# One step later for tanh, chunk 1's rows turned by transfers, weights requested and squared later (fused attention and MLP, one core)

## The chip, the cores and the metric

The kernel runs on one core of a Trainium2 chip. Its engines work side by side, each on its own list of instructions in order: PE (TensorE) multiplies matrices, ACT (ScalarE) and DVE (VectorE) work element by element, POOL (GpSimd) does small jobs, and SP (SyncE) issues most of the transfers. The metric is the device time of one execution in microseconds (us); lower is better.

## The reference, cut to what matters

```python
xn = layernorm(x)                                  # x: 2048 tokens x 640
q, k, v = split(xn @ wqkv)                         # 32 heads of 20
p = softmax(q @ k.T * 20 ** -0.5)                  # per head, 2048 x 2048
A = (p @ v).reshape(2048, 640) @ wo
h = gelu(layernorm(xn) @ w1 + b1)                  # 640 -> 1536, tanh form
out = x + A + h @ w2 + b2
```

## The kernel before

Everything is float32 in the reference. The kernel writes a float32 matrix as a sum of two 16-bit matrices (a "hi" and a "lo" part, after a scale that is a power of two), and multiplies with three matmuls: hi by hi, hi by lo, lo by hi (`PASS`). The scales come from sums of squares: ACT squares a weight matrix and adds up along the rows (L97, L464 for w2, L472 for w1, L483 for wo, L527 for Wq), PE multiplies the sums by a matrix of ones (`pow2`, L113), which adds over the 128 partitions, and a few one-column operations of DVE make a power of two of it (L114 to L119, L101, L423).

**Stage A, 0 to about 217 us**, takes the tokens in four chunks of 512 (c = 0 to 3). The order of the instructions is the one in which the program records them. For each chunk: its four tiles of 128 rows are loaded (`load_x`, L181); DVE takes mean and variance (`norm_a`, L243 to L245), scales the rows (`norm_b`, L258) and prepares the second layernorm's factor, which goes to a DRAM scratch, rscr (`norm_c`, L274). The rows are then turned, so that features lie on partitions, and split into hi and lo (xnt). For chunks 0 and 1, PE turns them (L537 and L541 for chunk 0; `transp`, L287, for chunk 1), and ACT and DVE copy them out of PSUM (L294, L295). For chunks 2 and 3 `turn` does it: ACT and DVE split the rows as they lie (L306, L307; three row buffers), and a DMA on SP transposes them (L308). SP stores each turned chunk to DRAM (xscr, L297 or L311) for the MLP.

With xnt, PE computes five tiles of q and k (`qk`, L325, 30 matmuls each), which ACT and DVE bring out of PSUM (L340, L341) and SP stores (qkscr, L346), and four tiles of v (`vproj`, L398; out by L408, L410). q, k and v tiles and the sums over partitions share three PSUM buffers (pool psS) in turn, so a tile waits until what stood in its buffer three allocations ago is read. In chunk 0 the columns of Wv are split (L431, L432) only after the fourth q/k tile.

Into this, two generators are cut in slices. `ask(n)` issues the next n loads of the MLP's weights on SP: six pieces of w2 of 640 KB, then five of w1 of 768 KB; chunk 0 asks for (0, 1, 2, 2, 1) behind its five q/k tiles and (2, 1, 1, 1) behind its four v tiles, and then for chunk 2's x. `some(n)` does the next n units of work on them: six squares of w2, scale "2", five squares of w1, scale "1", factors (with the square of b1), twelve splits of w2, fifteen of w1 (L128 to L130). In chunks 0 to 2 it does two behind each v tile, and in chunks 1 to 3 one or two behind each q/k tile.

**Stage B, from about 217 us,** is the attention. For each pair of heads, half of the queries and block of 128 keys, PE computes scores (L711), ACT takes the exponential (L713), DVE splits it where needed (L725), and PE multiplies by v (L742). After 16 blocks ACT evicts the sum (`ev`, L763), and transfers take it to DRAM. Between these, PE does the MLP (L976, L1006) and the projection by wo (z, L1090) as filler, by a credit in time. The element-wise work of the filler (gelu: a chain of DVE operations with a tanh on ACT) is a set of generators that advance by one step at every `tick`, two per group of four key blocks. `finish` turns the sums of a few heads into the attention's output: DVE adds up the denominators and takes reciprocals (L876 to L883), they are spread over the heads' rows, and DVE multiplies (L900 to L906); the result goes through DRAM (oscr) to the projection (ot, L1042).

**The tail** begins when the last scores are done, at about 1268 us. There are two chunks' worth of z matmuls left over, and `finish` for the last heads spreads the reciprocals with 32 matmuls (rb, L892), whose operand is not known until the last `ev` came back by a transfer. W1 sets how many ticks behind the loads the DVE chain and rb are recorded, a tick per three z matmuls; W2 how many ticks lie between rb and its reader (L900). The last 240 z matmuls (eight tiles of 30) read what this `finish` stores to oscr.

Of the kernel before, what the change touches and what calls it, by code (L numbers as in the profile page):

```python
# [9 lines left out]
F32 = mybir.dt.float32  # L10
# [8 lines left out]
P = 128  # L19
# [25 lines left out]
def mha_mlp_kernel(tc, x, wqkv, wo, w1, b1, w2, b2, out):  # L45
# [4 lines left out]
    with (  # L50
# [52 lines left out]

        def pow2(acc, tag):

            lo = keep.tile([P, 1], F32, name=f"lo_{tag}")
            hi = keep.tile([P, 1], F32, name=f"hi_{tag}")
            if tag in ("q", "k"):
                pt = psM.tile([P, 512], F32, tag="m", name="mxp")
            else:  # L110
                pt = psS.tile([P, 2, 512], F32, tag="s", name="mxp")[:, 0, :]
            n = acc.shape[1]
            nc.tensor.matmul(pt[:, :n], ones, acc, start=True, stop=True)  # L113
            nc.vector.tensor_reduce(lo, pt[:, :n], AX.X, ALU.add)  # L114
            nc.vector.tensor_scalar(lo, lo, 2.0**-100, 2.0**120, ALU.max, ALU.min)

            nc.vector.tensor_scalar(lo.bitcast(I32), lo.bitcast(I32), 0x7F000000, 1,
                                    ALU.bitwise_and, ALU.logical_shift_right)
            nc.vector.tensor_scalar(lo, lo, 2.0**64, None, ALU.mult)  # L119
            exponents(lo, hi)  # L120
            return lo, hi

        pw = {}

# [39 lines left out]
        with tc.tile_pool(name="pa", bufs=2) as pa, tc.tile_pool(name="pa1", bufs=1) as pa1, tc.manual_schedule():  # L164
# [21 lines left out]
            nc.gpsimd.memset(ones, 1.0)  # L186
            nc.gpsimd.memset(nhalf, -0.5)
            nc.gpsimd.memset(half, 0.5)
            load_x(0)
# [36 lines left out]
            def newton(dst, v, pref, by=1.0):  # L226
                t = pa.tile([P, 4], F32, tag=pref + "t", name=pref + "t")
                nc.vector.tensor_mul(t, dst, dst)
                nc.vector.tensor_mul(t, t, v)
                nc.vector.tensor_scalar(t, t, -0.5 * by, 1.5 * by, ALU.mult, ALU.add)  # L230
                nc.vector.tensor_mul(dst, dst, t)

            def norm_a(c, between=None):

                xt = xts[c]
                st = pa.tile([P, 4, 2, 6], F32, tag="st", name="st")
                mv = pa.tile([P, 4, 2], F32, tag="mv", name="mv")
                ve = pa.tile([P, 4], F32, tag="ve", name="ve")
                r = pa.tile([P, 4], F32, tag="r", name="r")
                r2 = pa.tile([P, 4], F32, tag="r2", name="r2")  # L240
                for j in range(4):
                    for i in range(2):
                        nc.vector.bn_stats(st[:, j, i, :], xt[j][:, i * 320 : (i + 1) * 320])  # L243
                    nc.vector.bn_aggr(mv[:, j, :], st[:, j])
                nc.vector.tensor_scalar(ve, mv[:, :, 1], EPS, None, ALU.add)  # L245
                if c == 0:
                    between()
                    nc.scalar.activation(r, ve, AF.Sqrt)
# [27 lines left out]
            xnts = {}  # L276

            def transp(c, k0, pts):
                if k0 == 0:
                    xnts[c] = pa.tile([P, KD, 2, 512], F16, tag="xnt", name=f"xnt{c}")  # L280
                if k0 + 2 > KD:
                    pt = psM.tile([P, 512], F32, tag="m", name="pt4")[:, None, :]
                else:
                    pt = psS.tile([P, 2, 512], F32, tag="s", name="pt")
                for j in range(4):
                    for k in range(min(2, KD - k0)):
                        nc.tensor.transpose(pt[:, k, j * P : (j + 1) * P],  # L287
                                            xts[c][j][:, (k0 + k) * P : (k0 + k + 1) * P], ident)
                pts.append((c, k0, pt))

            def transp_out(c, k0, pt):
                nk = min(2, KD - k0)
                ks = slice(k0, k0 + nk)
                nc.scalar.activation(xnts[c][:, ks, 0, :], pt[:, :nk], AF.Copy)  # L294
                nc.vector.tensor_sub(xnts[c][:, ks, 1, :], pt[:, :nk], xnts[c][:, ks, 0, :])  # L295
                if k0 + 2 > KD:
                    nc.sync.dma_start(xscr[:, :, :, c * 512 : (c + 1) * 512], xnts[c])  # L297
                    del xts[c]

# [114 lines left out]
            junk = pa1.tile([P, 3 * D], BF16, name="junk")  # L414
            accs, scales = {}, {}

            def sums(tag, ws):
                accs[tag] = squares(ws, junk)

            def scale_of(tag):  # L420
                pw[tag] = pow2(accs[tag], tag)
                scales[tag] = keep.tile([P, 1], F32, name=f"s_{tag}")
                nc.vector.tensor_scalar(scales[tag], pw[tag][1], 4096.0, None, ALU.mult)  # L423
                if tag in "qk":
                    q = "qk".index(tag)
                    nc.vector.tensor_scalar(qks[:, q : q + 1], pw[tag][0], QKTOP, 2.0**-22, ALU.min, ALU.mult)

# [93 lines left out]
            nc.scalar.activation(junk[:, :1], ones[:, :1], AF.Sqrt)  # L521
            warm(37)
            accs["q"] = sm.tile([P, 8], F32, tag="acc", name="acc")[:, :KD]
# [9 lines left out]
            pts = [psS.tile([P, 2, 512], F32, tag="s", name="pt") for _ in range(2)]  # L533
            pt = [pts[0][:, 0], pts[0][:, 1], pts[1][:, 0], pts[1][:, 1]]
            for j in range(4):
                for k in range(KD - 1):
                    nc.tensor.transpose(pt[k][:, j * P : (j + 1) * P], xts[0][j][:, k * P : (k + 1) * P], ident)  # L537
            scale_of("q")
# [3 lines left out]
            warm(3)  # L542

            for k in range(KD):
                nc.scalar.activation(xnts[0][:, k, 0, :], pt[k], AF.Copy)
                nc.vector.tensor_sub(xnts[0][:, k, 1, :], pt[k], xnts[0][:, k, 0, :])
                split_qkv("q", [k], 0, 2 * P)
            nc.sync.dma_start(xscr[:, :, :, :512], xnts[0])
            del xts[0]
            nc.gpsimd.dma_start(bscr[H : H + 1, :].rearrange("h (r t) -> h r t", r=4), brow[0:1, None, :].to_broadcast([1, 4, S // 4]))  # L550
            nc.gpsimd.dma_start(b1t, b1.rearrange("(k p) -> p k", p=P))
            for c in range(4):
                nxt = c + 1 if c < 3 else None
                for tt in range(5):
# [14 lines left out]
                    if c == 0:  # L569
# [22 lines left out]

                    ask((0, 1, 2, 2, 1)[tt] if c == 0 else 0)
                    if nxt and c > 0 and tt >= 2:
# [36 lines left out]
        with ExitStack() as scope:  # L631
# [278 lines left out]
            def gelu(ps, r2f, hT, f):  # L910
# [55 lines left out]
            def layer1(mc, f):  # L966
# [4 lines left out]
                for i in range(2):  # L971
                    n = 0
                    fo_ = (f + i) % 4 * P
                    for k in range(KD):
                        for a, b in PASS:
# [3 lines left out]
                            if n % 3 == 0:  # L979
                                if i == 1 and n == 15:  # L980
                                    begin(gelu(ps, r2f, hTs[mc], f))
                                yield 0.3276
# [72 lines left out]
            def ahead():  # L1055
# [3 lines left out]
                load_piece(0)  # L1059

            done = [False]
            ended = [False]
            W1, W2 = 10, 5

# [55 lines left out]
            with tc.manual_schedule():  # L1120
# [50 lines left out]
                n = 0  # L1171
                ended[0] = True
                fetch_results()
# [111 lines left out]
```

## Time and profile before

| | us |
|---|---|
| median of 3 runs | 1339.41 |
| lowest, highest | 1338.3, 1340.97 |
| the profiled execution | 1340.0 |
| its span, first to last instruction | 1338.0 |
| PE busy | 1328.0 |
| ACT busy | 1128.4 |
| DVE busy | 1055.1 |

The span is what the profile covers; about 2 us of the execution lie outside it. A group's row gives the busy time, the mean length of one instruction in ns and, behind the bar, the idle time of the engine ahead of it with what ended it. A row of the chain gives start, length, engine and line. A row of a table of windows gives, for each engine, busy time and instructions, then TensorE's granted clock, the DMA engines' busy share and GB/s. SPq and POOLq are transfers issued on those queues.

### The profile page before, as it was taken

How to read it: one execution, taken by the hardware profiler on the slowest of the kernel's cores; microseconds unless marked ns; L12 is line 12 of the kernel's file. 1: busy time of each engine (PE TensorE's matmuls, PEld its weight loads, DVE VectorE, ACT ScalarE, POOL GpSimd, SP SyncE). 2: the span in 40 equal slices, each digit the busy share in tenths (PEclk: the TensorE clock that was granted, in tenths of full speed). 3: DMA queues.
4: the chain of work that ended last, by engine and by line, in shares of the span. 5: the costliest groups of instructions: out<-in, count | busy, mean ns of one | idle time of the engine just before them, and what ended most of it. 6: DMA issues, size and time to landing. Idle time of an engine off the chain costs nothing.

```text
span 1338.0 us, 29071 instructions
## 1 busy us (share of the span) xinstructions
PE 1328.0 (99%) x11647; PEld 590.0 (44%) x11647; DVE 1055.1 (79%) x1436; ACT 1128.4 (84%) x1306; POOL 37.5 (3%) x85
## 2 busy tenths in 40 slices
PE   9999999999999999999999999999999999999998
PEld 6645545443434343444443444434343434333366
DVE  7767935998788888878897888898888888997632
ACT  7755525999999999999999999999999999999900
POOL 3011000000000000000000000000000000000000
PEclk9999999999999999999999999999999999999989
DMA  8767831121122223122322041322022323443465
GB/s 279 251 200 184 147 106 58 34 57 39 49 69 68 80 57 103 41 71 57 110 66 71 19 112 48 95 72 71 19 80 72 95 65 85 128 134 80 122 189 189
DMA packets 100150, 129.54 MB, mean 97 GB/s; under 512 B 24276, under 2 KB 66328, under 8 KB 100012
## 3 DMA queue, kind: packets, MB, share of 16 engines
q1 hardware_dynamic: 96652, 120.25, 30.7%
q0 software_dynamic: 2912, 6.90, 2.8%
q8 instruction: 92, 1.51, 0.5%
q10 hardware_dynamic: 448, 0.51, 0.2%
q14 instruction: 46, 0.38, 0.1%
HBM read 82.14 MB, written 42.51 MB: 93 GB/s over the span
## 4 chain that ended last, share of the span: by engine, by line
PE 96%; ACT 1%; DVE 1%; issue 1%; DMA 0%; ACTq 0%; POOL 0%; DVEq 0%; POOLq 0%
PE o L742 31%; PE s L711 20%; PE py L1006 13%; PE pu L976 12%; PE qkp L325 10%; PE vp L398 5%; PE z L1090 5%; PE warm L222 1%; ACT p L713 1%; DMA lt<-ev 0%; DVE low L725 0%; PE rb L892 0%; PE norms L370 0%; ACT ev L763 0%; PE pt L287 0%
## 5 line engine op out<-in xcount | busy, mean ns | idle before, releaser
L713 ACT ACTIVATE p<-s 128x1024 f32<-128x1024 f32 x1024 | 972.1, 1047 | 34.3 <-PE s L711 28.2
L725 DVE TENSOR_TENSOR low<-p 128x1024 f16<-128x1024 f32 x512 | 614.3, 1218 | 146.2 <-ACT p L713 145.2
L742 PE MATMUL o<-p,vfull 128*32 128x512 bf16 (+1 forms) x4096 | 429.0, 493 | 0.0
L711 PE MATMUL s<-qs,ks 61*128 61x512 f16 x2048 | 312.0, 381 | 1.3 <-ACT p L713 1.3
L711 PEld LDWEIGHTS <-ks 61*128 61x128 f16 x2048 | 61.1, 94 | 280.6 <-issue 279.0
L1006 PE MATMUL py<-w2t,hT 128*128 128x320 f16 x1152 | 178.5, 300 | 0.0
L976 PE MATMUL pu<-xm,w1t 128*128 128x256 f16 x1440 | 178.2, 273 | 0.0
L976 PEld LDWEIGHTS <-w1t 128*128 128x128 f16 x1440 | 131.0, 98 | 64.6 <-issue 51.0
L1006 PEld LDWEIGHTS <-hT 128*128 128x128 f16 x1152 | 102.3, 98 | 88.0 <-issue 53.9
L325 PE MATMUL qkp<-xnt,wv 128*128 128x512 f16 x600 | 131.1, 379 | 0.4 <-ACT vfull L408 0.2
L742 PEld LDWEIGHTS <-vfull 128*32 128x32 f16 x3072 | 59.7, 95 | 136.7 <-issue 105.3
L742 PE MATMUL o<-low,vfull 128*32 128x512 f16 x1024 | 101.1, 377 | 0.1
L325 PEld LDWEIGHTS <-wv 128*128 128x128 f16 x600 | 58.3, 98 | 70.0 <-DVE wv L432 1.1
L742 PEld LDWEIGHTS o<-p,vfull 128*32 128x32 f32 x2048 | 62.2, 108 | 53.1
L340 ACT ACTIVATE qkhl<-qkp,qks 128x1024 f16<-128x1024 f32 (+1 forms) x24 | 23.2, 966 | 55.4 <-PE qkp L325 35.7
L1090 PE MATMUL z<-w1t,ot 128*128 128x320 f16 x480 | 68.9, 304 | 0.0
L398 PE MATMUL vp<-wv,xnt 128*128 128x320 f16 x480 | 66.7, 299 | 0.0
L1090 PEld LDWEIGHTS <-ot 128*128 128x128 f16 x480 | 46.6, 99 | 23.9 <-issue 5.5
L398 PEld LDWEIGHTS <-xnt 128*128 128x128 f16 x480 | 46.7, 98 | 18.4
L341 DVE SCALAR_TENSOR_TENSOR qkhl<-qkp,qks,qkhl 128x1024 f16<-128x1024 f32 (+1 forms) x24 | 26.5, 1104 | 32.1 <-ACT qkhl L340 31.9
L1048 DVE SCALAR_TENSOR_TENSOR acc<-z,sc,acc 128x320 f32<-128x320 f32 x32 | 17.4, 545 | 42.2 <-PE z L1090 42.1
L996 POOL DMA_DIRECT2D xb<-in_B_b_dram x16 | 13.6, 849 | 986.7 <-DMA xb<-in_A_x_dram 429.8
(190 smaller groups left out, 701.7 us busy)
## 6 DMA issues: line engine op xcount, KB each, us to landing
qkscr<-qkhl SPq DMA_DIRECT2D x40, 256.0 KB
opart<-ev SPq DMA_DIRECT2D x124, 80.0 KB
ks<-qkscr SPq DMA_DIRECT2D x120, 80.0 KB
qs<-qkscr SPq DMA_DIRECT2D x192, 40.0 KB
oa<-opart SPq DMA_DIRECT2D x32, 240.0 KB
xt<-in_A_x_dram SPq DMA_DIRECT2D x16, 320.0 KB
xscr<-xnt SPq DMA_DIRECT2D x4, 1280.0 KB
xm<-xscr SPq DMA_DIRECT2D x8, 640.0 KB
```

The costliest lines, as they stand in the source:

```text
L325: nc.tensor.matmul(ps[:, i, :], wv[:, k, q, a, mm * P : (mm + 1) * P], xnts[c][:, k, b, :], start=(k + n == 0), stop=(k == KD - 1 and n == 2))
L340: nc.scalar.activation(hl[:, 0, i0:i1], ps[:, i0:i1], AF.Copy, scale=a)
L341: nc.vector.scalar_tensor_tensor(hl[:, 1, i0:i1], ps[:, i0:i1], a, hl[:, 0, i0:i1], ALU.mult, ALU.subtract)
L398: nc.tensor.matmul(ps[:, hf, :320], xnts[c][:, k, a, j * P : (j + 1) * P], wv[:, k, 2, b, hf * 320 : (hf + 1) * 320], start=(n == 0), stop ...
L711: nc.tensor.matmul(ps[:, a, :], ks[64 * a : 64 * a + 61, kb * P : (kb + 1) * P], qs[64 * a : 64 * a + 61, cc * 512 : (cc + 1) * 512], star ...
L713: nc.scalar.activation(pt, ps, AF.Exp, scale=QS)
L725: nc.vector.tensor_sub(low, pt, upper(pt))
L742: nc.tensor.matmul(pv.o[32 * q : 32 * q + 32, :], src[:, v0 - PAD * (1 - q % 2) :][:, :32], t, start=q not in pv.begun, stop=last, skip_gr ...
L976: nc.tensor.matmul(ps[:, i], w1v[:, k, (f + i) // 4, a, fo_ : fo_ + P], xnt[:, k, b, :], start=(n == 0), stop=(n == 3 * KD - 1))
L1006: nc.tensor.matmul(ps[:, :320], hTs[mc][:, f, a, j * P : (j + 1) * P], w2v[:, f, b, hf * 320 : (hf + 1) * 320], start=(n == 0), stop=(n == ...
L1048: nc.vector.scalar_tensor_tensor(acc[:, cols], ps[:, :320], fo, acc[:, cols], ALU.mult, ALU.add)
L1090: nc.tensor.matmul(ps[:, :320], ot[:, k, a, j * P : (j + 1) * P], wov[:, k, b, h * 320 : (h + 1) * 320], start=(n == 0), stop=(n == 3 * KD ...
```

## The change

Six things change together.

1. *Head.* The five partial sums of Wq's squares are multiplied by ones one column at a time, as they come, adding up in PSUM (`add_squares`), where before one matmul did it at the end and DVE added the columns. The scale for q is made in four DVE operations (six before); the rest (`whole`, `back`) is done later. 32 warming matmuls (25, 3 and 4) stand where there were 37, and two where there were three. `newton` has three DVE operations (four before), and the first square root takes its epsilon as a bias.
2. *Chunk 1's rows* are turned by `turn`, as those of chunks 2 and 3: rows 0 and 1 behind the split of Wv, rows 2 and 3 and `norm_c(1)` behind the last q/k tile of chunk 0. `norm_b(1)` moves ahead of the split of Wv. `transp`, `transp_out` are gone.
3. *Requests:* (0, 1, 2, 0, 0) behind the q/k tiles and two behind each v tile of chunk 0. By the order of SP's instructions, three pieces of w2 stand ahead of the first transpose; the other three, five of w1 and chunk 2's x stand behind the store of chunk 1 to xscr, which waits for all four transposes.
4. *Units:* one behind each v tile of chunk 0; 2, 2, 2, 0 in chunks 1 and 2; and the eviction of a v tile is recorded ahead of the units (behind them before). By ACT's order, the last three squares of w2 now stand right ahead of chunk 1's first q/k eviction, and the last square of w1 right behind the eviction of chunk 1's first v tile. On DVE, the reduction of scale "2" stands right behind the statistics of chunk 2's rows.
5. *Tanh:* where an eviction `ev` is recorded in the same group, gelu pauses one tick before its tanh, so that ACT has ev and two exponentials ahead of the tanh. A gelu that is still going on is finished before the next begins.
6. *Tail:* W1 is 18 (10 before): 144 z matmuls of the leftover stand ahead of rb, 120 before.

```diff
+            if tag == "q":
+                scales[tag] = keep.tile([P, 1], F32, name=f"s_{tag}")
+                nc.vector.tensor_scalar(hi.bitcast(I32), lo.bitcast(I32), 0x3F800000, None, ALU.bitwise_xor)
+                nc.vector.tensor_scalar(scales[tag], hi, 2.0**76, None, ALU.mult)
+                return lo, hi
...
-            warm(37)
+            warm(25)
...
+            pq = psM.tile([P, 512], F32, tag="m", name="mxq")
+            def add_squares(i):
+                nc.tensor.matmul(pq[:, :1], ones, accs["q"][:, i : i + 1], start=i == 0, stop=i == KD - 1)
+            add_squares(0)
+            warm(3)
+            add_squares(1)
+            warm(4)
...
                         elif tt == 3:
                             scale_of("v")
+                            norm_b(1)
                             split_qkv("v")
+                            turn(1, 0)
+                            turn(1, 1)
...
-                    ask((0, 1, 2, 2, 1)[tt] if c == 0 else 0)
+                    ask((0, 1, 2, 0, 0)[tt] if c == 0 else 0)
+                    if c == 0 and tt == 4:
+                        turn(1, 2)
+                        turn(1, 3)
+                        norm_c(1)
...
-                    if c == 0:
-                        if j < 2:
-                            (norm_b, norm_c)[j](1)
-                        pts = []
-                        for k in ((), (0,), (2, 4), ())[j]:
-                            transp(1, k, pts)
-                        for t in pts:
-                            transp_out(*t)
+                    if c + j > 0:
+                        vproj_out(c, j, ps)
...
-                    some(2 if c < 3 else 1)
-                    vproj_out(c, j, ps)
+                    some(1 if c in (0, 3) else 2 if j < 3 else 0)
+                    if c + j == 0:
+                        vproj_out(c, j, ps)
                     if c == 0:
-                        ask(2 if j == 0 else 1)
+                        ask(2)
...
+                if reading[0]:
+                    yield
                 nc.scalar.activation(w, w, AF.Tanh, scale=0.7978845608028654 * 0.044715)
...
-            W1, W2 = 10, 5
+            W1, W2 = 18, 5
...
+                        reading[0] = kb % GRP > 1 and prev is not None and prev[-1][3] == NKB - 1
                         tick()
```

More of the change, by code (lines that the diff above doesn't have):

```diff
@@ L102, in exponents, with pow2, whole @@
                                     ALU.bitwise_and, ALU.bitwise_xor)
-        def pow2(acc, tag):
+        def pow2(acc, tag, total=None):
             lo = keep.tile([P, 1], F32, name=f"lo_{tag}")
             hi = keep.tile([P, 1], F32, name=f"hi_{tag}")
[L108 to L115, printed above, removed]
+            if total is None:
+                if tag == "k":
+                    pt = psM.tile([P, 512], F32, tag="m", name="mxp")
+                else:
+                    pt = psS.tile([P, 2, 512], F32, tag="s", name="mxp")[:, 0, :]
+                n = acc.shape[1]
+                nc.tensor.matmul(pt[:, :n], ones, acc, start=True, stop=True)
+                nc.vector.tensor_reduce(lo, pt[:, :n], AX.X, ALU.add)
+                total = lo
+            nc.vector.tensor_scalar(lo, total, 2.0**-100, 2.0**120, ALU.max, ALU.min)
             nc.vector.tensor_scalar(lo.bitcast(I32), lo.bitcast(I32), 0x7F000000, 1,
                                     ALU.bitwise_and, ALU.logical_shift_right)
+            if tag == "q":
[3 more added lines that the diff above has]
+                return lo, hi
+            whole(lo, hi)
+            return lo, hi
+        def whole(lo, hi):
             nc.vector.tensor_scalar(lo, lo, 2.0**64, None, ALU.mult)
             exponents(lo, hi)
-            return lo, hi
-        pw = {}
+        pw, scales = {}, {}
         def split(pool, src, h, l, scale, n):
@@ L187, in mha_mlp_kernel @@
             nc.gpsimd.memset(nhalf, -0.5)
+            eps = keep.tile([P, 1], F32, name="eps")
+            nc.gpsimd.memset(eps, EPS)
             nc.gpsimd.memset(half, 0.5)
@@ L228, in newton @@
                 nc.vector.tensor_mul(t, dst, dst)
-                nc.vector.tensor_mul(t, t, v)
-                nc.vector.tensor_scalar(t, t, -0.5 * by, 1.5 * by, ALU.mult, ALU.add)
-                nc.vector.tensor_mul(dst, dst, t)
+                nc.vector.scalar_tensor_tensor(t, v, -0.5 * by, t, ALU.mult, ALU.mult)
+                nc.vector.scalar_tensor_tensor(dst, t, 1.5 * by, dst, ALU.add, ALU.mult)
             def norm_a(c, between=None):
@@ L247, in norm_a @@
                     between()
-                    nc.scalar.activation(r, ve, AF.Sqrt)
+                    nc.scalar.activation(r, mv[:, :, 1], AF.Sqrt, bias=eps)
                     nc.vector.reciprocal(r, r)
@@ L276, in mha_mlp_kernel @@
             xnts = {}
[L278 to L298, printed above, removed]
             def turn(c, j):
@@ L414, in mha_mlp_kernel, with scale_of, back @@
             junk = pa1.tile([P, 3 * D], BF16, name="junk")
-            accs, scales = {}, {}
+            accs = {}
             def sums(tag, ws):
                 accs[tag] = squares(ws, junk)
[L420 to L426, printed above, removed]
+            def scale_of(tag, total=None):
+                pw[tag] = pow2(accs[tag], tag, total)
+                if tag not in scales:
+                    scales[tag] = keep.tile([P, 1], F32, name=f"s_{tag}")
+                    nc.vector.tensor_scalar(scales[tag], pw[tag][1], 4096.0, None, ALU.mult)
+                if tag == "k":
+                    back(tag)
+            def back(tag):
+                if tag == "q":
+                    whole(*pw[tag])
+                q = "qk".index(tag)
+                nc.vector.tensor_scalar(qks[:, q : q + 1], pw[tag][0], QKTOP, 2.0**-22, ALU.min, ALU.mult)
             def split_qkv(n, ks=range(KD), c0=0, c1=D):
@@ L537, in mha_mlp_kernel @@
                     nc.tensor.transpose(pt[k][:, j * P : (j + 1) * P], xts[0][j][:, k * P : (k + 1) * P], ident)
-            scale_of("q")
+                if j in (0, 2):
+                    add_squares(2 + j // 2)
+            add_squares(4)
+            scale_of("q", pq[:, :1])
             pt.append(psM.tile([P, 512], F32, tag="m", name="pt4"))
@@ L541, in mha_mlp_kernel @@
                 nc.tensor.transpose(pt[4][:, j * P : (j + 1) * P], xts[0][j][:, 4 * P :], ident)
-            warm(3)
+            warm(2)
             for k in range(KD):
@@ L547, in mha_mlp_kernel @@
                 split_qkv("q", [k], 0, 2 * P)
+            back("q")
             nc.sync.dma_start(xscr[:, :, :, :512], xnts[0])
@@ L980, in layer1 @@
                                 if i == 1 and n == 15:
-                                    begin(gelu(ps, r2f, hTs[mc], f))
+                                    for it in [it for it in sides if it is active[0]]:
+                                        for _ in it:
+                                            pass
+                                        sides.remove(it)
+                                    active[0] = gelu(ps, r2f, hTs[mc], f)
+                                    begin(active[0])
                                 yield 0.3276
@@ L1059, in ahead @@
                 load_piece(0)
+            reading = [False]
+            active = [None]
             done = [False]
             ended = [False]
-            W1, W2 = 10, 5
+            W1, W2 = 18, 5
             def projection():
@@ L1171, in mha_mlp_kernel @@
                 n = 0
+                reading[0] = False
                 ended[0] = True
```

## The prediction

> **What bounds the kernel now.** I read the page first, then the waits of TensorE (PE), then the chain from 40 to 112 us and the last 60 us, and only then the transfers.
>
> ```profile
> span 1338.0 us, 29071 instructions
> PE 1328.0 (99%) x11647; PEld 590.0 (44%) x11647; DVE 1055.1 (79%) x1436; ACT 1128.4 (84%) x1306; POOL 37.5 (3%) x85
> ...
> L711 PE MATMUL s<-qs,ks 61*128 61x512 f16 x2048 | 312.0, 381 | 1.3 <-ACT p L713 1.3
> ```
> PE is busy for 1328.0 of 1338.0 us, and in the attention it waits 1.3 us in all. The profiled execution took 1340.0 us, 2 us outside its span; the median of the runs is 1339.41. All sums below are differences on that trace, put on the median. What is worth something is a PE instruction less, or one of the few PE waits; every new wait costs its full length. The largest wait is near the end:
>
> ```profile
> PE rb L892 <- DVE lt L883: 2.2, 1, 2.2
> ```
> ```profile
> 1268.00:1276.20 8.20, 8.20 (x68) 4.97 (x65) 1.65 (x3) 0.60 (x1) 0.71 (x1) 1.00 0.68 210
> 1276.20:1278.40 2.20, 0.04 (x1) 0.00 (x0) 1.19 (x6) 0.00 (x0) 0.00 (x0) 1.00 0.38 105
> ...
> 1278.90:1285.70 6.80, 6.80 (x41) 5.33 (x40) 0.00 (x0) 0.00 (x0) 0.00 (x0) 0.50 0.81 237
> ```
> In these windows the seventh entry (ahead of the DMA share) is the granted clock. After 2.2 us of idling PE works for 6.8 us at half clock, which costs 6.8/2 = 3.4 us more.
>
> **The change, part by part.** First what stands in chunk 1, where most of it happens.
>
> ```profile
> 48.92 8.15 PE vp L398 x60
> ...
> 57.52 1.02 PE pt L287 x8
> 58.54 4.08 PE vp L398 x30
> 62.61 0.89 PE pt L287 x8
> ...
> 68.32 26.06 PE qkp L325 x120
> ```
> ```profile
> L287 PE MATMUL pt<-ident,xt 128*128 128x128 f32 x20 | 2.6, 275 | 0.0
> ```
> *Transposes out:* 20 matmuls, 2.6 us busy; they overlap a little, so I take −2.4.
>
> *Head:* the sum of Wq's squares is gathered on PE while PE would warm up, and the chain to the scale has two VectorE (DVE) steps less.
> ```profile
> 13.72 0.16 DVE L114 TENSOR_REDUCE lo_q<-mxp 128x1 f32<-128x5 f32 x1 [1.03 <-PE mxp L113]
> ...
> 14.67 0.15 DVE L423 TENSOR_SCALAR s_q<-hi_q 128x1 f32<-128x1 f32 x1
> ```
> Five intervals take 0.95 us, so one step is 0.19 and two are 0.38: −0.35. The later warming passes fill time in which PE waits anyway.
>
> *New waits in chunk 0:* DVE now normalises chunk 1 ahead of splitting Wv's columns, and subtracts two turned rows ahead of a q/k eviction.
> ```profile
> L258 DVE TENSOR_SCALAR xt<-xt,mv,r 128x640 f32<-128x640 f32 x16 | 8.7, 608 | 0.1
> ...
> L307 DVE TENSOR_TENSOR row<-xt,row 128x640 f16<-128x640 f32 x8 | 6.4, 818 | 0.0
> ...
> L432 DVE SCALAR_TENSOR_TENSOR wv<-w1t,s_v,wv 128x640 f16<-128x640 f32 x5 | 4.1, 878 | 0.9 <-ACT wv L431 0.9
> ```
> ```profile
> 43.40 0.15 DVE L423 TENSOR_SCALAR s_v<-hi_v 128x1 f32<-128x1 f32 x1
> ```
> From 43.55: newton 0.6, four normalisations 2.2, three small steps 0.6, five splits 4.1: 51.0. The first v tile, at 48.92 before and earlier by the head, reads the last split some 2 us in, at about 50.7 (+0.35); the second needs a buffer whose eviction is 1.5 us later by the two rows (+0.55). Both lie between 0 and 1.2.
>
> *The turned rows and what is queued behind them.* DVE goes on: two rows 1.6, two evictions 2.5, two rows 1.6: the fourth row is ready at about 57. On SP the four transposes stand among the q/k stores.
> ```profile
> L308 SPq DMA_TRANSPOSE xnt<-row x4: 1361/2426/5132, 93.4 to 108.6; - x4
> ```
> At the shortest issue (1.36 us each) the fourth is out by 59 and landed by about 61.5; chunk 1's first q/k matmul wants it at 66. Then SP waits for all four, and only behind that come the store of chunk 1, three w2 pieces, five w1 pieces, and chunk 2's x:
> ```profile
> xt<-in_A_x_dram SPq DMA_DIRECT2D x16, 320.0 KB
> xscr<-xnt SPq DMA_DIRECT2D x4, 1280.0 KB
> ...
> w2t<-in_B_w_dram SPq DMA_DIRECT2D x6, 640.0 KB
> w1t<-in_B_w_dram SPq DMA_DIRECT2D x5, 768.0 KB
> ...
> wos<-in_A_wo_dram POOLq DMA_DIRECT2D x5, 320.0 KB, 3.9
> ```
> 1280 + 3×640 + 5×768 + 4×320 KB are 8.52 MB. The rate comes from windows (last column GB/s):
> ```profile
> 28.00:32.00 4.00, 4.00 (x20) 1.80 (x19) 4.00 (x9) 4.00 (x9) 0.00 (x0) 1.00 0.88 93
> ...
> 58.00:64.00 6.00, 6.00 (x49) 4.83 (x48) 2.51 (x5) 4.71 (x7) 0.79 (x1) 1.00 1.04 418
> ...
> 72.00:80.00 8.00, 8.00 (x39) 3.63 (x38) 1.95 (x3) 4.09 (x5) 0.00 (x0) 1.00 1.03 402
> ...
> 96.00:104.00 8.00, 8.00 (x47) 4.46 (x46) 6.15 (x24) 2.86 (x6) 0.00 (x0) 1.00 1.04 85
> ```
> At about 410 GB/s (402 and 418) it is 20.8 us; a lone 320 KB load takes 3.9 us of which 0.8 is data, so 3.1 of latency. Landing: 61.5 + 3.1 + 20.8 = 85.4. To that comes a stretch in which the queues are busy and move almost nothing (93 and 85 GB/s); such stretches begin 3 to 5 us after the write of r to rscr:
> ```profile
> L274 POOL DMA_DIRECT2D rscr<-r x3: 791/791/817, 25.3 to 93.9; - x3
> ...
> DMA to landing us min/median/max: 9.6/10.0/10.4
> ```
> In the changed kernel the write goes out at 57.5, so the stretch falls on 61 to 66. It costs (402−93)/402×4 = 3.1 us by the window at 28 and 6.3 by that at 96; below, nothing, if it falls elsewhere. I take 3.1, the nearer in what is in flight (no transposes): x lands at 88.5.
>
> Who waits for x? DVE's statistics of chunk 2, and in DVE's order behind them the reduction of scale "2", whose PSUM buffer the fourth q/k tile of chunk 1 takes over.
> ```profile
> 79.93 0.89 DVE L243 BATCH_NORM_STATS2 st<-xt 128x6 f32<-128x320 f32 x2 [1.91 <-DMA xt<-in_A_x_dram]
> ...
> 84.07 0.17 DVE L245 TENSOR_SCALAR ve<-mv 128x4 f32<-128x4 f32 x1
> ```
> One tile's statistics take 1.0 us, so the reduction is through 1.5 us after the last tile: 90.0. Before, the fourth tile began at 68.32 + 26.06×3/4 = 87.9; now PE is there at 87.9 − 0.35 − 2.4 + 0.9 = 86.0. So it waits 4.0 us, and everything earlier, gains too, ends at that transfer: **+2.1** against before (0 to +3.2 more with the longer stretch, −3.1 less without). An idle PE of 4 us is longer than the 2.2 of the end, so I let it lose the clock the same way: **+3.4**.
>
> The Trainium skill ("TensorE: Matmul & The Clock Gate", Part 1) says that the clock halves after a whole idle window of 3.4 us, and that windows run freely. Here 2.2 us were enough, so the trace disagrees with the letter of it; a 4 us wait would mostly keep its clock by that rule, and the sum would be 5 us lower.
>
> *Scale "1":* the last square of W1 now stands on ACT behind the eviction of v tile (1,0), and PE's sum over it right behind that tile.
> ```profile
> L408 ACT ACTIVATE vfull<-vp 128x640 f16<-128x640 f32 (+1 forms) x16 | 11.1, 693 | 15.9 <-PE vp L398 15.9
> ...
> L472 ACT ACTIVATE junk<-w1t 128x1536 bf16<-128x1536 f32 x5 | 7.4, 1478 | 1.2 <-DMA w1t<-in_B_w_dram 1.2
> ```
> PE idles 0.69 + 1.48 + 0.2 for the accumulator less overlap = **+2.3**, with no cover: PE has nothing else queued. Whether that loses the clock too is open (0 or 3.4): half, **+1.7**. The sum for b1 one tile later waits likewise for an eviction and a short square: **+0.7**. The rest of the weights' squares and splits moves later, into ACT's idle time of chunks 2 and 3: 0.
>
> *Attention:* tanh stands behind an eviction and the exponentials it would have delayed, at some ten places. PE's waits there are 1.3 in all, so −1.3 to +1 (an eviction of gelu late); **−0.5**.
>
> *Tail:* 24 more z matmuls stand ahead of rb, 24×0.136 = 3.3 us, against an idle of 2.2: the wait goes (−2.2), and with it the half clock (−3.4). What is late next:
> ```profile
> 1278.48 4.13 PE L892 MATMUL rb<-lt,sel 64*80 64x64 f32 x32 [2.24 <-DVE lt L883]
> ...
> 1291.28 0.40 ACTq L907 DMA_DIRECT2D oscr<-oa  x1
> ...
> 1294.63 1.14 SPq L1042 DMA_DIRECT2D ot<-oscr  x2
> ```
> DVE's chain behind rb starts with the z tile at 1286.3, which comes 4 us earlier, so oscr goes out 3.3 us earlier, while the last chunk's z, its reader, wants ot 5.6 us earlier. Before, oscr took 3.3 us to land (1291.28 to ot's issue at 1294.63), and ot's two transfers, issued up to 1295.8, by the same measure landed at 1298 to 1299; the last chunk's z began at 1282.6 + 12×0.27 + 108×0.136 = 1300.5. So 1.5 to 2.5 us were to spare, and 2.3 are now used: 0 to 0.8 late by this, up to 1.4 if a landing takes longer, I take 0.6. Tail: **−5.0** (−2.2 if the clock falls all the same, −5.6 at best).
>
> Sum: 2.1 + 3.4 + 2.3 + 1.7 + 0.7 − 0.5 − 5.0 = **+4.7**: 1344.1, say 1344.
>
> **The rivals.**
> 1. *The forecast*, chunk 1's wait for x with a halved clock: 1341.5 to 1347. For it: the volume queued behind one wait, and the order on DVE. Against: 4 us out of a 27 us queue is within what I can read. 0.40.
> 2. *Slow stretch on the transposes themselves.* If the write to rscr hits before the fourth row is landed, it lands at 66 to 68, the queue follows, x lands at 93 to 95 and PE stands twice: 5 to 7 us more, 1350. For it: one such transpose of before took 5.1 us to issue, in that stretch. Against: the write goes out when the fourth row is already out. 0.12.
> 3. *x comes in time (the other side, faster).* If x is landed by 84.5, DVE is through by 86 and PE never waits there: −1.9 instead of +2.1 and no lost clock; with 2.3 + 0.7 − 0.5 − 5.0, and the clock kept at scale "1", −4.4: 1335. It decides at 84.5: queues that begin 1 us earlier and no slow stretch are enough. 0.21.
> 4. *The wait is there, but the clock stays* (short waits, or windows that split them): 2.1 + 2.3 + 0.7 − 0.5 − 5.0 = −0.4, 1339; 1337 to 1341. That is also what the skill's rule gives. Against: the 2.2 us of the tail. 0.19.
> 5. *The tail doesn't do what it is meant to*: rb no longer waits, but a late ot stops PE as long as before and the clock falls: 2.8 us over the forecast, 1347. 0.08.
>
> **How the numbers follow.** A measurement here can tell about 0.2%, 2.7 us. Faster: rival 3 and a tenth of 4, 0.22. Same: most of 4 and the lower edge of 1, 0.21. Slower: the rest, 0.57. The range leaves out a tenth below (rival 3's lower half) and a tenth above (most of rival 2): 1334 to 1350. The likeliest case by itself spans 1341.5 to 1347.
>
> **What would show it.** Right: a PE wait of 2 to 6 us at about 86, put down to DVE's scale reduction, with x's landing ahead of DVE's statistics at 87 to 90; a half clock behind it; a PE wait of about 2.3 at about 108, put down to ACT's square of W1; no wait and clock 1.00 where rb stands. Wrong: statistics that start before 83, a fourth row that lands after 64, a clock of 1.00 throughout chunk 1, or PE waits of over 2 us in the last 45 us.

## The result, and the profile after

The changed kernel takes 1358.48 us (1357.9 to 1360.12, 4 runs), the kernel before in the same runs 1339.16: a ratio of 1.0133, with a 95% interval of 1.0121 to 1.0145. It is 19.3 us slower; the forecast was 4.7 slower, with a range up to 1350. The span of the profiled execution grew from 1338.0 to 1356.4, by 18.4.

From the page after:

```profile
span 1356.4 us, 29022 instructions
PE 1329.5 (98%) x11623; PEld 586.8 (43%) x11623; DVE 1054.8 (78%) x1429; ACT 1128.3 (83%) x1307; POOL 38.1 (3%) x86
...
L724 PE MATMUL s<-qs,ks 61*128 61x512 f16 x2048 | 311.2, 381 | 0.1
...
L1027 PE MATMUL py<-w2t,hT 128*128 128x320 f16 x1152 | 178.5, 300 | 1.8 <-DVE u L927 1.8
```

PE's busy time is nearly the same (1329.5 against 1328.0, with fewer matmuls but more of them at half clock). What was added is waiting. PE's waits after, from the whole span (us in all, times, longest; line numbers are those of the changed kernel: L315 the q/k tiles, L114 the sums over the partitions, L1027 the MLP's second layer, L1113 z):

```profile
PE qkp L315 <- DMA xnt<-row: 5.5, 1, 5.5
PE qkp L315 <- DVE lo L115: 5.4, 1, 5.4
PE mxp L114 <- ACT junk L469: 5.3, 1, 5.3
PE py L1027 <- DVE u L927: 1.8, 2, 0.9
...
PE qkp L315 <- DVE qkhl L331: 0.9, 1, 0.9
PE z L1113 <- DMA ot<-oscr: 0.6, 1, 0.6
PE mxp L114 <- ACT junk L97: 0.5, 1, 0.5
```

The first three stand within 55 us of each other, in chunk 1: ahead of its first q/k tile, ahead of its fourth, and ahead of the sum over the squares of W1. By the starts of PE's tiles in the two traces, the changed kernel is 2.0 us ahead when chunk 0 is done, 3.5 behind when chunk 1 begins (68.32 before, 71.82 after), 11.7 at its fourth q/k tile (87.74, 99.43) and 21.9 at chunk 2 (118.36, 140.28). Chunks 2 and 3 change nothing. The attention adds 1.1 (from the first scores to the last 1047.1 before, 1048.2 after), and the tail gives 4.6 back (from the last product with v to the end 68.97 before, 64.38 after).

The chain from 40 to 140 us shows what the three waits wait for (start, length):

```profile
58.96 12.66 DMA xnt<-row
...
72.28 7.96 DMA w2t<-in_B_w_dram
80.26 14.73 DMA xt<-in_A_x_dram
...
108.90 11.83 DMA xnt<-row
...
122.14 1.47 ACT junk L469 x2
```

The fourth transpose of chunk 1 is issued at 59.0, as forecast, and lands (is reported done) at 71.6, ten microseconds after the 61.5 of the forecast. The write of r to rscr in this stretch, and windows of the same execution (PE's clock and the DMA engines' share are the seventh and eighth entries):

```profile
L286 POOL DMA_DIRECT2D rscr<-r x1: 791/791/791, 57.5 to 57.5; - x1
...
DMA to landing us min/median/max: 13.3/13.3/13.3
```
```profile
58.00:64.00 6.00, 6.00 (x52) 4.32 (x45) 1.74 (x4) 3.38 (x5) 0.32 (x1) 1.00 1.05 166
64.00:71.60 7.60, 2.37 (x18) 1.47 (x15) 0.00 (x0) 0.99 (x3) 0.00 (x0) 0.98 0.00 0
71.60:74.00 2.40, 2.18 (x6) 0.81 (x7) 0.00 (x0) 0.00 (x0) 0.00 (x0) 0.50 0.47 157
...
99.40:104.00 4.60, 4.57 (x16) 1.82 (x16) 4.34 (x13) 0.13 (x1) 1.03 (x1) 0.71 0.16 57
...
124.00:132.00 8.00, 7.46 (x57) 4.41 (x57) 1.81 (x9) 1.06 (x4) 0.00 (x0) 0.66 0.85 201
```

Two things are to be seen. From 64 to 71.6 no byte moves (share 0.00, 0 GB/s), and yet the transposes are not reported done: the write, issued at 57.5, lands 13.3 us later, at 70.8, and the fourth transpose right behind it. And behind each of the three waits of over 5 us the clock is below 1.00: 0.50, 0.71 and 0.66.

Theory A, then: the write of r as 512 pieces of four bytes holds up the completion of the transposes that are in flight with it. Rival B: the transposes are slow by themselves, behind the four stores.

### The profile page after: what moved, and what is told of

Its sections match the earlier page's. It is cut to its first block, busy times and chain, and to the rows that moved or that the text cites. A ratio compares the mean times of both kernels' runs of the same rounds, so it can differ in the third digit from the quotient of the medians.

```text
span 1356.4 us, 29022 instructions
## 1 busy us (share of the span) xinstructions
PE 1329.5 (98%) x11623; PEld 586.8 (43%) x11623; DVE 1054.8 (78%) x1429; ACT 1128.3 (83%) x1307; POOL 38.1 (3%) x86
## 4 chain that ended last, share of the span: by engine, by line
PE 90%; DMA 4%; DVE 3%; ACT 1%; issue 1%; SPq 0%; POOL 0%; ACTq 0%; DVEq 0%; POOLq 0%
PE o L755 30%; PE s L724 20%; PE py L1027 13%; PE pu L991 12%; PE qkp L315 7%; PE z L1113 4%; PE vp L388 4%; DMA xnt<-row 2%; DMA xt<-in_A_x_dram 1%; PE warm L235 1%; ACT p L726 1%; DMA w2t<-in_B_w_dram 1%; DVE low L738 1%; DMA ot<-oscr 0%; DMA oscr<-oa 0%
## 5 line engine op out<-in xcount | busy, mean ns | idle before, releaser
L1027 PE MATMUL py<-w2t,hT 128*128 128x320 f16 x1152 | 178.5, 300 | 1.8 <-DVE u L927 1.8
L315 PE MATMUL qkp<-xnt,wv 128*128 128x512 f16 x600 | 134.1, 384 | 11.8 <-DMA xnt<-row 5.5
L1027 PEld LDWEIGHTS <-hT 128*128 128x128 f16 x1152 | 102.4, 98 | 89.8 <-issue 55.6
L315 PEld LDWEIGHTS <-wv 128*128 128x128 f16 x600 | 58.8, 99 | 83.8 <-issue 16.1
L388 PE MATMUL vp<-wv,xnt 128*128 128x320 f16 x480 | 69.7, 306 | 0.3 <-DVE qkhl L331 0.2
L1113 PE MATMUL z<-w1t,ot 128*128 128x320 f16 x480 | 67.6, 299 | 0.6 <-DMA ot<-oscr 0.6
L1113 PEld LDWEIGHTS <-ot 128*128 128x128 f16 x480 | 45.9, 98 | 23.7 <-issue 5.5
L398 ACT ACTIVATE vfull<-vp 128x640 f16<-128x640 f32 (+1 forms) x16 | 11.3, 704 | 37.1 <-PE vp L388 37.1
```

The source lines that it names most:

```text
L315: nc.tensor.matmul(ps[:, i, :], wv[:, k, q, a, mm * P : (mm + 1) * P], xnts[c][:, k, b, :], start=(k + n == 0), stop=(k == KD - 1 and n == 2))
L388: nc.tensor.matmul(ps[:, hf, :320], xnts[c][:, k, a, j * P : (j + 1) * P], wv[:, k, 2, b, hf * 320 : (hf + 1) * 320], start=(n == 0), stop ...
L1027: nc.tensor.matmul(ps[:, :320], hTs[mc][:, f, a, j * P : (j + 1) * P], w2v[:, f, b, hf * 320 : (hf + 1) * 320], start=(n == 0), stop=(n == ...
L1113: nc.tensor.matmul(ps[:, :320], ot[:, k, a, j * P : (j + 1) * P], wov[:, k, b, h * 320 : (h + 1) * 320], start=(n == 0), stop=(n == 3 * KD ...
```

## The experiments

**The write in fewer pieces.** Same place, same bytes. The factors of the second layernorm land on other tokens.

```diff
-                nc.gpsimd.dma_start(rscr[c * 512 : (c + 1) * 512].rearrange("(j p) -> p j", p=P), r2)
+                nc.gpsimd.dma_start(rscr[c * 512 : (c + 1) * 512].rearrange("(p j) -> p j", p=P), r2)
```

> The changed kernel, but the layernorm factor goes to rscr as 128 pieces of 16 bytes instead of 512 of 4 bytes (in another order, so the second layernorm's factors land on other tokens); its place in the program is the same. Theory A: the write of 4-byte pieces holds up the transposes that are in flight with it until it has landed itself (in the changed kernel it lands at 70.8 us, the fourth transpose at 71.7, though the last packet of both is through at 64). Then a write in flight for a quarter as many pieces lands sooner: the fourth row is there by 65, PE's wait of 5.5 us ahead of chunk 1 falls below 1, the wait of 5.4 at the fourth q/k tile below 2, and that of 5.3 for the square of W1 to about 2.3; 1343 to 1348. Rival B: the transposes are slow of themselves behind four stores and land at 71 whatever the write is: 1358, the same waits. Rival C: the write's landing time does not go by its number of pieces: as B in time, but the write still lands just ahead of the transposes.

Measured: 1347.68 (1345.07 to 1348.75), 1.0033 of before (1.0018 to 1.0047), at the upper end of the 1343 to 1348 expected. The write's landing times of the four chunks, and PE's longest waits:

```profile
L286 POOL DMA_DIRECT2D rscr<-r x4: 546/590/607, 25.4 to 146.9; - x4
...
DMA to landing us min/median/max: 2.5/5.6/6.9
```
```profile
PE qkp L315 <- DVE lo L115: 5.6, 1, 5.6
PE mxp L114 <- ACT junk L469: 2.3, 1, 2.3
```
The chain has the fourth transpose out at 59.2 and done 4.85 us later:
```profile
59.16 4.85 DMA xnt<-row
```
The wait ahead of chunk 1 is gone, that for the square of W1 is 2.3 instead of 5.3, by the forecast's own sum; only the wait at the fourth tile stays, where below 2 was expected. Chunk 1 now costs 11.6 us against before instead of 21.9. B and C fall: the transposes are quick, and the write in flight with them lands 6.0 us after its issue instead of 13.3.

**The write at another time**, in four-byte pieces as before, when the chunk's transposes are through. The short DVE operations that prepare the factor move with it.

```diff
                         turn(1, 3)
-                        norm_c(1)
...
-                            (norm_a, norm_b, norm_c)[step](nxt)
+                            (norm_a, norm_b, lambda c: None)[step](nxt)
...
                     qk_out(c, tt, ps)
+                    if c > 0 and tt == 0:
+                        norm_c(c)
```

> The changed kernel with the write to rscr of chunks 1 to 3 moved behind the first q/k tile of the same chunk, when its transposes have landed; nothing else moves. Theory A: chunk 1's fourth row lands at about 64, PE's wait ahead of chunk 1 falls from 5.5 to 0, and the write now falls on the loads (issue near 74), so that x of chunk 2 comes at 88 to 95 instead of 95; the transposes of chunk 2 are free of it, so PE's wait for the square of W1 falls from 5.3 to 2.3: 1345 to 1352. Rival B (transposes slow by themselves): landing stays near 71, waits stay, 1357 to 1359.

Measured: 1352.9 (1351.64 to 1356.5), 1.0087 (1.0064 to 1.011), a little above the 1345 to 1352 expected. From the chain, and from PE's waits:

```profile
59.04 4.84 DMA xnt<-row
...
72.56 21.07 DMA xt<-in_A_x_dram
```
```profile
PE qkp L315 <- DVE lo L115: 11.8, 1, 11.8
PE mxp L114 <- ACT junk L469: 2.3, 1, 2.3
```
The transposes take 4.84 us, as with the smaller write: by themselves they were never slow. The write now falls on the loads, and x of chunk 2 comes 21.1 us behind w2's third late piece instead of 14.7. Here, too, the two land together: the write goes out at 80.9 and lands 12.5 us later, at 93.4, and x lands at 72.56 + 21.07 = 93.6. So the transposes of the changed kernel were late by 7.8 us (12.66 against 4.84), and x here by 6.3, each beside this write.

**Chunk 2's x first** (with the 16-byte write, whose factors land on other tokens):

```diff
+                if j == 3 and c == 1:
+                    load_x(2)
                 if j == 3:
                     nc.sync.dma_start(xscr[:, :, :, c * 512 : (c + 1) * 512], xnts[c])
...
-                if c == 0:
-                    load_x(2)
```

> The run with the 16-byte write (its factors land on other tokens), and besides chunk 2's x is requested right behind the fourth transpose, ahead of the store of chunk 1 and of the eight pieces of w2 and w1 that stood before it. There, PE waited 5.6 us at the fourth q/k tile for DVE's scale reduction, behind chunk 2's statistics. Theory: that wait is the queue ahead of x. Then x lands near 70, DVE's statistics no longer wait, and the wait falls below 1; the three pieces of w2 come 3.2 us later and ACT, which squares them ahead of chunk 1's first eviction, now holds PE at the third tile for 0 to 3 us. 5 to 8 us faster than the 16-byte run on the same chip or against the same before. Rival: DVE is late there for its own work (evictions, statistics): the wait stays above 4.

Measured: 1342.79 (1341.5 to 1344.22), 1.0017 (1.0001 to 1.0034). By the spans of the two profiled executions (1341.6 and 1346.5) it is 4.9 faster than with the 16-byte write alone; by the medians against the kernel before that ran beside each it is 3.5 faster (2.3 slower than before instead of 5.8). Expected were 5 to 8.

```profile
PE mxp L114 <- ACT junk L471: 2.3, 1, 2.3
PE qkp L317 <- DVE qkhl L333: 1.9, 1, 1.9
```
The wait at the fourth tile is gone: it was the queue ahead of x and not DVE's own work. In its place stands 1.9 at the third tile, where ACT squares the late pieces of w2 first, within the 0 to 3 that was named.

**The tail alone**, in the kernel before:

```diff
-            W1, W2 = 10, 5
+            W1, W2 = 18, 5
```

> The kernel before with 24 more z matmuls ahead of rb (W1 18) and nothing else. The tail's part of the sum alone: PE's wait of 2.2 ahead of rb and the half clock of 6.8 us behind it go, a wait of 0.6 for ot comes: 4.6 us faster, 1334.6 (between 1333.5 and 1335.5). If the half clock did not come from the wait, only 2.2 faster: 1337.

Measured: 1342.0 (1339.74 to 1343.39), before beside it 1341.91, 1.0 (0.9987 to 1.0012): no gain, where 4.6 was expected. Against the trace of before, the tail itself does what it should, 64.51 us from the last product to the end instead of 68.97, with no wait ahead of rb. But at the start of chunk 2 this execution is 4.8 us behind, in a program that has not changed there:

```profile
99.40 13.77 SPq L308 DMA_TRANSPOSE xnt<-row  x2
...
111.58 0.74 ACT L306 ACTIVATE row<-xt 128x640 f16<-128x640 f32 x1 [8.57 <-DMA xnt<-row]
```
```profile
PE qkp L325 <- DVE vfull L410: 2.2, 1, 2.2
PE vp L398 <- DVE vfull L410: 1.8, 1, 1.8
```
Its writes landed after 11.2 to 13.3 us, where those of the first profile took 9.6 to 10.8. So the kernel before has the same fault with no slack to spare: in the execution whose writes take about 10 us, ACT's wait for a transpose of chunk 2 is 1.4 and PE's is nothing; in this one, they are 8.6 and 4.0. That does not explain the missing gain, because the runs of before beside it have the same write, and no trace shows where their time goes. Why the tail is worth nothing here stays open.

**The factor as rows**, alone and with the tail. PE turns the factor, and four rows of 512 bytes are written:

```diff
+                pt = psM.tile([P, 512], F32, tag="m", name="ptr")
+                nc.tensor.transpose(pt[:4, :P], r2, ident)
+                rr = pa.tile([4, P], F32, tag="rr", name="rr", bufs=1)
+                nc.vector.tensor_copy(rr, pt[:4, :P])
+                nc.gpsimd.dma_start(rscr[c * 512 : (c + 1) * 512].rearrange("(j p) -> j p", p=P), rr)
...
+                    if c < 3 and j == (3 if c == 0 else 2):
+                        rows_out(c + 1)
```

The write also goes out later with this edit: by the traces of before and of the rows alone, chunk 1's at 69.0 instead of 58.8, and chunk 2's at 117.0 instead of 93.9, when that chunk's transposes are out.

> The kernel before with the factor written as rows of 512 bytes and nothing else. Theory: level with before where its write is quick (1338 to 1339), and up to 4.8 faster than before where before loses time to it; the spread of the runs narrows. Rival: no change in either.

> The kernel before with two things: the factor is turned on PE (a 128 x 4 transpose) and written to rscr as four rows of 512 bytes, and W1 is 18. A full computation. Theory: on this kind of chip the write of 4-byte pieces takes 10 to 14 us and holds chunk 2's transposes, which costs the kernel before nothing where it takes 10 (as in its profile) and up to 4.8 where it takes 13 (as in the run of the tail alone). With rows it lands within 4 us: no wait in chunks 1 to 3, and the tail's 4.5 less: 1333 to 1335, whatever the chip. Rival (the write's form doesn't matter): as the tail alone, level with before.

Measured: alone 1339.71 (1336.12 to 1340.63), 0.9992 (0.9975 to 1.0009); with the tail 1337.42 (1336.56 to 1338.53), 0.9979 (0.9965 to 0.9992). The kernel before ran from 1335.19 to 1344.47 beside them. The spread narrows as expected and PE has no wait in chunks 1 to 3 in either; alone it is level by the median, and with the tail the gain is 3.1 us by the medians and ends above the 1333 to 1335 expected, in part because ot came 1.9 us late there. The writes landed 2.3 to 7.2 us after their issue, where 4 at most was expected. Since form and time change together, these two runs don't tell which of them frees chunk 2's transposes.

**Tanh back**, in the changed kernel:

```diff
-                if reading[0]:
-                    yield
                 nc.scalar.activation(w, w, AF.Tanh, scale=0.7978845608028654 * 0.044715)
```

> The changed kernel with tanh back in its old place. The changed kernel loses 1.1 us between the first and the last scores (1025.2 from 239.85 to 1265.04 became 1048.2 to 1288.0, with two waits of 0.9 of the second layer for gelu's last step). If the later tanh is the cause, these waits go and the run is 1.0 to 1.9 faster than the changed kernel (1356.6 to 1357.5); if they come from the shift of the stage against the transfers, it stays within 0.5 of 1358.5.

(The lengths in that text are a slip: before it is 1047.1, from 217.94.) Measured: 1357.84 (1356.97 to 1358.69), and the changed kernel did not run beside it, so the times don't tell 0.6 us; by the traces the attention takes 1046.7 instead of 1048.2, and the two waits of 0.9 are gone.

**All of it rebuilt**: the changed kernel with the factor as rows (and its write later), x first, tanh back, and the squares in later slots.

```diff
-                            some(1)
-                        else:
-                            some(2)
+                        some((0, 1, 1, 1, 2)[tt] if c == 1 else 2)
...
-                    some(1 if c in (0, 3) else 2 if j < 3 else 0)
+                    some(((1, 1, 1, 0), (2, 2, 1, 0), (2, 2, 2, 2), (1, 1, 1, 1))[c][j])
```

> The changed kernel rebuilt after what the runs show: factor written as rows of 512 bytes, chunk 2's x requested right behind the fourth transpose, the squares of w2 and w1 in later slots so that none stands right ahead of the sum that PE takes of it, tanh in its old place. A full computation. Theory: chunk 1's PE waits for transfers and squares go (below 1.5 in all), 20 transposes stay out: 2 us ahead of the kernel before at the start of chunk 2, and the tail 4.5: 1331 to 1334. Rival: moving weights about brings a new wait in chunks 1 to 3 of 2 us or more: 1334 to 1340, and where it stands is seen in the waits.

Measured: 1333.8 (1333.48 to 1334.78), 0.9948 (0.9931 to 0.9965), within the 1331 to 1334 expected and faster than both kernels. All of PE's waits over 0.5 us in its span:

```profile
PE mxq L548 <- ACT junk L536: 1.1, 1, 1.1
PE warm L235 <- POOL ones L197: 1.1, 1, 1.1
PE s L736 <- ACT p L738: 1.1, 3, 0.4
PE z L1123 <- DMA ot<-oscr: 0.8, 1, 0.8
```
Nothing of chunk 1 is left in them. At chunk 2 it is 1.8 us ahead of the kernel before in this trace (116.58 against 118.36), and 2.3 in the trace of the same kernel taken again (116.03). That is what the whole change of chunks 0 and 1 is worth once nothing waits; no run has the turning by transfers alone.

**Tanh and W1 in the rebuilt kernel**, three kernels on one chip:

> The rebuilt kernel again, as the common base of the two runs beside it: 1333 to 1335, by the same steps as before.

> The rebuilt kernel with the later tanh put in again, nothing else. By the traces of the changed kernel with and without it, the attention is 1.5 us longer with it, two waits of 0.9 of the second layer for gelu's last step: 1.0 to 1.8 slower than the rebuilt kernel. The view of the prediction (the later tanh takes waits of PE away) wants 0.5 to 1.3 faster.

> The rebuilt kernel with 120 z matmuls ahead of rb, as in the kernel before. By the prediction's terms 2.2 slower by the wait alone, and 5.0 where the clock also falls behind it. In the run with the factor as rows alone the times stand in two heaps, at 1336.3 and 1340, so the clock seems to fall only in some of the executions: two heaps 3 to 4 apart, at about 1335.5 and 1339. If it falls in all, one heap at 1338 to 1339; if the heaps have another cause, the rebuilt kernel shows them too.

Measured: the base 1333.7 (1333.27 to 1333.96); with the later tanh 1335.6 (1334.78 to 1336.32); with W1 10, 1336.72 (1334.28 to 1340.8). The later tanh costs 1.9, a little over what was expected, with the same two waits:

```profile
PE py L1039 <- DVE u L939: 1.8, 2, 0.9
```
W1 is worth 3.0 by the medians; its runs lie not in two heaps but spread over 6.5 us, and their mean clock falls with the time, from 1.000 at 1334.28 to 0.996 at 1340.8. In the profiled run with W1 10:

```profile
PE rb L917 <- DVE lt L908: 1.5, 1, 1.5
```
```profile
1275.00:1280.00 5.00, 4.19 (x39) 3.42 (x40) 1.04 (x3) 0.00 (x0) 0.00 (x0) 0.79 0.78 245
1280.00:1285.00 5.00, 5.00 (x33) 3.41 (x32) 2.88 (x3) 0.00 (x0) 0.00 (x0) 0.86 0.53 160
```
Here a wait of 1.5 is followed by a lower clock. That the clock is what spreads the others fits their mean clocks; there is no trace of them.

## Why the prediction was wrong

The sign was right, and so was the place: chunk 1, PE behind DVE's scale reduction behind chunk 2's x. The size was not: +4.7 forecast, +19.3 measured. By stage, in the pair of traces: chunks 0 and 1 were put at +10.2 (2.1 + 3.4 + 2.3 + 1.7 + 0.7) and took 21.9 more; the attention −0.5 and +1.1; the tail −5.0 and −4.6.

- **The step that failed** is the fourth transpose "landed by about 61.5", and with it the wait for x that the sum builds on it. The prediction's own signs of being wrong name it: "a fourth row that lands after 64". The transpose needs 4.85 us from its issue with nothing in the way, which makes 64, so 2.5 us were missing from the start; the other 7.6 come from the write to rscr, for the transpose lands only when that has landed (70.8, then 71.6). The prediction had the write's 10 us in a row in front of it, and read it as a stretch in which the queues move little, to be charged at 3.1 us to the loads. It is a hold on completion: bytes can still move (418 GB/s from 58 to 64 in the trace of before, whose write goes out at 58.8), but the transposes are reported done only when the write has landed. In the trace of before the write of chunk 2 lands at 93.9 + 10 = 104, and ACT, waiting for a transpose, goes on just then; that coincidence was there to be seen:

```profile
104.09 0.74 ACT L306 ACTIVATE row<-xt 128x640 f16<-128x640 f32 x1 [1.36 <-DMA xnt<-row]
```
The rival with a chance of 0.12 had the mechanism, with a landing of 66 to 68 and a sum of 1350, so it too was short.
- *The load queue's size was right.* From the moment SP was let go (71.7), the store, the weights and x took 23.3 us to land (95.0); the forecast's 3.1 + 20.8 for 8.52 MB is 23.9. So x came 6.5 us later than the 88.5 of the forecast because SP was let go 10.2 later; the 3.1 charged for the slow stretch did not come on top. At the fourth tile PE is 11.7 behind, where +2.1 was put.
- *Scale "1": +2.3 forecast, 5.3 measured.* The sum 0.69 + 1.48 + 0.2 is right to a tenth: 2.3 in the three runs in which nothing holds the transposes. Missing was that ACT has the last row of chunk 2 ahead of that eviction, with three row buffers, so that it waits for a transpose which the next write holds (109.6 + 11.0 = 120.6; ACT goes on at 120.8).
- *The clock.* +3.4 and +1.7 were put in. After the waits of 5.5, 5.4 and 5.3 it was below 1.00, and the windows give 1.2 (half of 2.4 us), 1.3 (0.29 of 4.6) and 2.7 (0.34 of 8), and another 0.4 from 74 to 78 (clock 0.91): about 5.6 in all. That this is near the 5.1 put in is luck: there are three waits of over 5 us where two of 4.0 and 2.3 were counted, and the first of them was not forecast.
- *Chunk 0* came out by its sum, 2.0 ahead at its end against 0.35 + 2.4 − 0.9 = 1.85, partly by luck. PE's new waits are about 0.5 instead of 0.9 (one of 0.2, and 0.3 in the first v tile: 4.47 us for 30 matmuls, where 60 took 8.31 in the kernel before). *The head* gave nothing (the first q/k tile at 15.46, before 15.42): DVE has two operations less, but the last of the five small matmuls now ends later, behind the transposes of x:

```profile
13.82 0.28 PE L536 MATMUL mxq<-acc,ones 128*128 128x1 f32 x2
...
14.71 0.15 DVE L125 TENSOR_SCALAR s_q<-hi_q 128x1 f32<-128x1 f32 x1
```
The scale is ready at 14.71 + 0.15, as before at 14.67 + 0.15.
- *Tanh: −0.5 forecast, +1.1 measured*, +1.9 by itself. It removes 1.2 us of waits for the exponentials (1.3 before, 0.1 after), but gelu then ends too late for the second layer, which waits 1.8. These waits come to +0.6; the rest is not explained.
- *The tail: −5.0 forecast, −4.6 in this pair of traces.* The wait and the half clock are gone:

```profile
1302.40:1306.40 4.00, 4.00 (x45) 3.50 (x45) 0.52 (x2) 0.00 (x0) 0.00 (x0) 1.00 0.92 249
```
Over many executions it is worth less by the medians: 3.0 in the rebuilt kernel, 2.3 between the two runs with rows, nothing in the kernel before. With W1 10 the mean clock differs from one execution to the next (1.000 to 0.996), so part of the −5.0 is not there in each of them. In the list of rivals, the fifth is priced 2.8 over the forecast; by its own condition, a stop as long as before and the clock lost, it takes back all 5.0.

Not settled: why the write takes 9.6 to 10.8 us in the profile of before and 10.7 to 14.0 in the others with 4-byte pieces, and whether it is DRAM or the DMA engines that make the others wait for it. No run separates these.

## What to carry to other kernels

A transfer of many tiny pieces is priced by its time to landing, and what is in flight beside it may be reported done only then; look for other transfers that land just when it does. When a transfer takes an engine's place in a chain, look at what else is in flight at that time, and at which loads are queued behind its completion on the issuing queue. A PE gap of a few microseconds can cost more than its length, so a wait that has no cover is to be priced with and without the clock behind it.

## What the runs showed of the hardware

- A write of 512 pieces of 4 bytes from 128 partitions landed 9.6 to 14.0 us after its issue; the same 2 KB as 128 pieces of 16 bytes 2.5 to 6.9, as four rows of 512 bytes (issued later in the kernel) 1.6 to 7.5. The Trainium skill ("DMA: Bandwidth & Descriptors", Specifications) gives 512 bytes as the least for full rate, with a read-modify-write below it. The runs agree in direction, but 16 bytes gain nearly as much as 512, which that limit does not say.
- The queues can show no traffic for 7.6 us (64.0 to 71.6) while transposes whose last packet is through are not yet reported done. Beside a write of 4-byte pieces, transposes landed just behind it (70.8 and 71.6, 120.6 and 120.7), and so did a load (93.4 and 93.6).
- The clock fell after PE waits of 5.5, 5.4, 5.3 and 2.2 us, and after one of 1.5. Two waits of 2.2 and 1.8 in the run of the tail alone left it at 1.00. The Trainium skill ("TensorE: Matmul & The Clock Gate", Part 1) asks for a whole idle window of about 3.4 us, on a window that runs freely. The runs agree that gaps of the same length can cost differently (2.2 us: 6.8 us at half clock in one trace, none in another), and disagree on the least length.
